# Seven quarter products in place of eight for the out-projection of an attention and feed-forward kernel on one Trainium2 core

## The chip, the cores and the metric

The kernel runs on one core of one Trainium2 chip. The metric is the device time of one execution in microseconds (us), median of several. The four executions of the kernel before took 314.61 to 314.81 us (0.06% apart). A profile records every instruction of one execution on the core's engines: PE (TensorE, matrix multiply; PEld is its weight loads), DVE (VectorE), ACT (ScalarE), POOL (GpSimd) and SP (SyncE, which here only issues DMA).

Each engine works through its own instructions in the order in which the program gives them: in the trace of the changed kernel all instructions that come from its list of words (3198 matmuls on PE, 419 instructions on DVE, 317 on ACT, 176 on POOL) start in the list's order on their engine.

## The reference

```python
def attention(q, k, v):                  # batch 8, heads 8, 576 tokens, head size 64
    scores = q @ k.T / sqrt(64)
    mask = (rel >= 0) & (rel < 64)       # sliding window, causal
    return softmax(where(mask, scores, -1e9)) @ v

def ffn(x, w_in, w_out):                 # x: 4608 x 512, w_in: 512 x 2048, w_out: 2048 x 512
    h = maximum(x @ w_in, 0)
    return (h * h) @ w_out

out = ffn(attention(q, k, v).transpose(0, 2, 1, 3).reshape(4608, 512), w_in, w_out)
```

All inputs and the output are float32; the kernels multiply fp16 and keep the products' sums in float32 tiles.

## The kernel before

The 4608 tokens are nine groups (0 to 8) of 512. A group is four chunks of 128 tokens for attention, then one up-projection of 16 slices (128 rows of h each), then one out-projection. A long list of short words gives the order of all steps on all engines; a letter after @ names the engine. The words that matter here:

- `S E M V N` (chunk): scores on PE, exponential on ACT, mask on DVE, value product on PE, normalisation on DVE.
- `U R Q` (chunk, quarter) in groups 0 and 1, `u r s` (group, slice) from group 2: up-projection on PE, relu on ACT, square.
- `O Z z`: a quarter of a token block's out-projection on PE (4 matmuls of 512 columns), eviction from PSUM (the memory that PE's results land in) on ACT, store.

```python
def up(g, f):                                   # word u: one slice, 4 matmuls of 512 columns
    hps = live["U", g, f] = ps_up.tile([P, 512], FP32, ...)      # 2 PSUM buffers
    for c in range(DMC):
        nc.tensor.matmul(hps[:], w_in_q[f // 4][:, c, ...], xT_of(g)[:, :, c, :], ...)

def relu(key, a, b):                            # words R, r
    nc.scalar.activation(out=hrelu, in_=hps[:], func=AF.Relu, scale=H_SCALE)

def square(key, a, b):                          # words Q, s: reads PSUM again, always on DVE
    nc.vector.scalar_tensor_tensor(
        out=out, in0=hps[:], scalar=0.0, in1=hr, op0=ALU.max, op1=ALU.mult)

def out_proj(g, ts, fq):                        # word O
    for f in range(4):
        nc.tensor.matmul(
            live["o", g, ts][:], h2s["h", g][:, 4 * fq + f, ts * P:(ts + 1) * P],
            w_out_q[fq][:, f, :], ...)
# ... loads, casts, attention, evictions and stores left out
```

The softmax here doesn't subtract the row's maximum and nothing guards it: scores larger than these inputs give would overflow.

## Time and profile before

| | before |
|---|---|
| time, median of 4 runs | 314.63 us (314.61 to 314.81) |
| PE, DVE, ACT, POOL busy | 95%, 59%, 52%, 32% |
| chain of waits | 81% PE |

The table of stretches of the kernel before: start and end of the stretch in us, its length, then the busy us and the instructions of PE, PEld, DVE, ACT and POOL, the granted share of PE's clock, the DMA engines' busy share and GB/s.

```profile
40.00:60.00 20.00, 18.30 (x247) 10.94 (x246) 14.21 (x34) 13.12 (x21) 9.03 (x13) 1.00 1.08 262
60.00:80.00 20.00, 18.86 (x331) 14.55 (x329) 15.19 (x36) 11.73 (x22) 8.34 (x13) 1.00 1.00 181
80.00:100.00 20.00, 18.95 (x219) 10.76 (x216) 13.68 (x27) 11.35 (x21) 10.68 (x17) 1.00 1.20 217
100.00:130.00 30.00, 28.63 (x257) 13.40 (x257) 20.61 (x46) 16.00 (x29) 11.27 (x18) 1.00 1.03 187
130.00:300.00 170.00, 170.00 (x1251) 79.14 (x1250) 92.96 (x191) 82.81 (x144) 43.42 (x69) 1.00 0.73 157
```

From 130 us PE is busy in every microsecond and is the bound. From 40 to 130 us it has small idle gaps, 5.3 us in all. Two lines of the chain of waits (start, length, what) near the end give what a matmul costs when nothing holds it up:

```profile
295.46 10.36 PE ops L440 x48
305.82 3.51 PE ops L466 x32
```

The 48 matmuls have 512 columns: 215.8 ns each. The 32 have 256 columns: 109.7 ns each. Halving the columns loses almost nothing (two of 256 take 219.4 ns, one of 512 215.8), although every matmul loads its own weights (98 ns each, on PEld beside PE). Four groups of instructions matter for the change (line, engine, operation, shapes, count; busy us and mean ns of one; idle time of the engine just before them and what ended it):

```profile
L426 DVE SCALAR_TENSOR_TENSOR h<-hps,hrelu 128x512 f16<-128x512 f32 x144 | 98.6, 689 | 86.6 <-ACT hrelu L413 86.1
L440 PE MATMUL ops<-w_out,h 128*128 128x512 f16 x560 | 140.9, 380 | 0.2 <-DVE h L426 0.2
L405 PE MATMUL hps<-xT,w_in 128*128 128x512 f16 x448 | 114.4, 380 | 1.1 <-DVE h L426 1.1
L413 ACT ACTIVATE hrelu<-hps 128x512 f32<-128x512 f32 x144 | 85.7, 599 | 97.6 <-PE hps L405 85.0
```

A warning on "PE busy": the records of matmuls overlap. The mean of one of 512 columns is 380 ns (its end is modelled by the profile), while 48 in a row took 215.8 ns each, so 380 ns is not what one costs. To see PE's real losses I add up, over the blocks of matmuls in program order, the time from one block's first matmul to the next block's first, less what the block takes at the rates above (and at the rates that blocks of other shapes show where nothing holds them up). I call the sum **PE's lost time**. It counts waits and half-clock time alike. Before, it is 26.1 us.

### The profile page before, as it was taken

How to read it: one execution, taken by the hardware profiler on the slowest of the kernel's cores; microseconds unless marked ns; L12 is line 12 of the kernel's file. 1: busy time of each engine (PE TensorE's matmuls, PEld its weight loads, DVE VectorE, ACT ScalarE, POOL GpSimd, SP SyncE). 2: the span in 40 equal slices, each digit the busy share in tenths (PEclk: the TensorE clock that was granted, in tenths of full speed). 3: DMA queues.
4: the chain of work that ended last, by engine and by line, in shares of the span. 5: the costliest groups of instructions: out<-in, count | busy, mean ns of one | idle time of the engine just before them, and what ended most of it. 6: DMA issues, size and time to landing. Idle time of an engine off the chain costs nothing.

```text
span 312.6 us, 7115 instructions
## 1 busy us (share of the span) xinstructions
PE 297.4 (95%) x2830; PEld 160.6 (51%) x2830; DVE 184.6 (59%) x402; ACT 163.4 (52%) x280; POOL 98.6 (32%) x157
## 2 busy tenths in 40 slices
PE   7599989989998999999999999999999999999995
PEld 3479844857844444444544444444444444444444
DVE  3788668596559647745764576557654855343400
ACT  2768784764556446445554565356535553444311
POOL 3443326263346216425723541333225200000000
PEclk9769999999999999999999999999999999999999
DMA  7999999899999999999989999999998022111221
GB/s 236 306 361 378 364 257 332 191 191 158 241 200 181 169 191 247 167 222 232 225 182 207 235 203 207 227 224 217 197 222 189 34 69 67 36 34 34 53 85 67
DMA packets 155569, 59.71 MB, mean 191 GB/s; under 512 B 140560, under 2 KB 146960, under 8 KB 155536
## 3 DMA queue, kind: packets, MB, share of 16 engines
q1 hardware_dynamic: 155536, 59.26, 84.1%
q8 instruction: 22, 0.36, 0.5%
q14 instruction: 11, 0.09, 0.1%
HBM read 38.80 MB, written 9.44 MB: 154 GB/s over the span
## 4 chain that ended last, share of the span: by engine, by line
PE 81%; DVE 11%; DMA 3%; ACT 2%; issue 1%; POOL 0%; SPq 0%; ACTq 0%
PE ops L440 35%; PE hps L405 29%; PE hps L396 8%; DVE pm L342 5%; PE av L353 3%; DMA kq_st<-in_q_dram 3%; PE sc L327 3%; DVE x_sb L364 2%; DVE h L426 2%; PE run_ps L285 2%; PE ops L466 1%; ACT pm L336 1%; DVE qT L291 1%; DVE rden L363 1%; ACT hrelu L413 1%
## 5 line engine op out<-in xcount | busy, mean ns | idle before, releaser
L426 DVE SCALAR_TENSOR_TENSOR h<-hps,hrelu 128x512 f16<-128x512 f32 x144 | 98.6, 689 | 86.6 <-ACT hrelu L413 86.1
L440 PE MATMUL ops<-w_out,h 128*128 128x512 f16 x560 | 140.9, 380 | 0.2 <-DVE h L426 0.2
L413 ACT ACTIVATE hrelu<-hps 128x512 f32<-128x512 f32 x144 | 85.7, 599 | 97.6 <-PE hps L405 85.0
L405 PE MATMUL hps<-xT,w_in 128*128 128x512 f16 x448 | 114.4, 380 | 1.1 <-DVE h L426 1.1
L440 PEld LDWEIGHTS <-h 128*128 128x128 f16 x560 | 52.4, 98 | 59.6 <-DVE h L426 0.3
L405 PEld LDWEIGHTS <-w_in 128*128 128x128 f16 x448 | 42.6, 98 | 51.6 <-issue 2.0
L336 ACT ACTIVATE pm<-sc 128x512 f16<-128x512 f32 x72 | 38.5, 602 | 12.8 <-PE sc L327 12.0
L270 POOL CAST v_ev<-st 128x512 f16<-128x512 f32 x31 | 19.4, 626 | 60.0 <-DMA st<-in_v_dram 27.9
L396 PE MATMUL hps<-xT,w_in 128*128 128x128 f16 x512 | 31.9, 223 | 1.1 <-DVE h L426 1.1
L364 DVE TENSOR_TENSOR x_sb<-av,rden 128x256 f16<-128x256 f32 x72 | 30.6, 425 | 2.5
L396 PEld LDWEIGHTS <-w_in 128*128 128x128 f16 x512 | 30.0, 100 | 3.3 <-issue 1.4
L448 ACT ACTIVATE osb<-ops 128x512 f32<-128x512 f32 x35 | 20.9, 600 | 18.9 <-PE ops L440 18.9
L342 DVE TENSOR_TENSOR pm<-pm,mask_inner 128x512 f16<-128x512 f16 x56 | 27.6, 523 | 0.1
L259 POOL CAST q<-st 128x512 f16<-128x512 f32 x24 | 14.9, 619 | 30.6 <-DMA st<-in_q_dram 29.5
L259 POOL CAST k<-st 128x512 f16<-128x512 f32 x28 | 17.4, 638 | 15.4 <-DMA st<-in_k_dram 15.0
L353 PEld LDWEIGHTS <-pm 128*64 128x64 f16 x576 | 13.2, 113 | 15.4 <-issue 7.8
L274 POOL COPY v_od<-v_ev 64x512 f16<-64x512 f16 x24 | 16.0, 666 | 8.1 <-DVE v_ev L270 3.7
L353 PE MATMUL av<-v_ev,pm 128*64 128x65 f16 x384 | 17.5, 202 | 0.4 <-DVE pm L342 0.2
L327 PE MATMUL sc<-qT,kT 64*128 64x64 f16 x576 | 15.2, 196 | 2.8 <-ACT qT L291 1.3
L278 POOL COPY v_od<-v_ev 64x512 f16<-64x512 f16 x24 | 15.3, 636 | 8.0 <-PE hps L396 3.5
L363 DVE RECIPROCAL rden<-av 128x4 f32<-128x4 f32 x72 | 12.6, 175 | 7.7 <-PE av L353 7.5
L327 PEld LDWEIGHTS <-kT 64*128 64x128 f16 x576 | 11.2, 98 | 8.6 <-issue 7.2
(49 smaller groups left out, 105.6 us busy)
## 6 DMA issues: line engine op xcount, KB each, us to landing
st<-in_v_dram SPq DMA_DIRECT2D x40, 256.0 KB, 4.3
out_dram<-osb SPq DMA_DIRECT2D x31, 256.0 KB, 3.2
st<-in_k_dram SPq DMA_DIRECT2D x28, 256.0 KB, 4.8
st<-in_q_dram SPq DMA_DIRECT2D x20, 256.0 KB, 4.5
w_st<-in_moe_w_in_dram SPq DMA_DIRECT2D x4, 1024.0 KB, 10.0
w_st<-in_moe_w_out_dram SPq DMA_DIRECT2D x4, 1024.0 KB, 9.8
kq_st<-in_k_dram SPq DMA_DIRECT2D x3, 1024.0 KB, 7.7
kq_st<-in_q_dram SPq DMA_DIRECT2D x3, 1024.0 KB, 9.4
```

The lines of the kernel that those rows point to most:

```text
L259: copier(e)(out=kq16(key, i // 4)[:, :, i % 4, :].rearrange("p a (b d) -> p a b d", d=D), in_=st[key, i][:].rearrange("p (a b) d -> p a b ...
L327: nc.tensor.matmul(sc[hh][:, hp, blk, :], kT[r0:r0 + 64, hp, a0:a0 + P], qTs["q", g][r0:r0 + 64, hp, a + 64 * blk:a + 64 * blk + 64], star ...
L336: nc.scalar.activation(out=pm[:], in_=live["s", i][hh][:], func=AF.Exp, scale=1.0 / float(D) ** 0.5)
L342: nc.vector.tensor_tensor(out=pms[i, hh][:], in0=pms[i, hh][:], in1=mask[:], op=ALU.min)
L353: nc.tensor.matmul(av[64 * blk:64 * blk + 64, h % 4, 0:65], pms[i, h % 2][:, h // 2, blk, :], vv[:, h, 0:65], start=True, stop=True)
L364: nc.vector.tensor_tensor(out=xs[i // 2][:, 2 * half:2 * half + 2, i % 2, :].rearrange("p c (b d) -> p c b d", d=D), in0=av[:, :, 0:D].rea ...
L396: nc.tensor.matmul(hps[:, f, :], w_in_q[fq][:, c, f * P:(f + 1) * P], xT_of(i // 4)[:, i % 4 // 2, c, a:a + P], start=(c == 0), stop=(c == ...
L405: nc.tensor.matmul(hps[:], w_in_q[f // 4][:, c, f % 4 * P:(f % 4 + 1) * P], xT_of(g)[:, :, c, :], start=(c == 0), stop=(c == DMC - 1))
L413: nc.scalar.activation(out=hrelu[:] if key == "U" else hrelu[:].rearrange("p (f t) -> p f t", t=P), in_=hps[:], func=AF.Relu, scale=H_SCALE)
L426: nc.vector.scalar_tensor_tensor(out=out, in0=hps[:], scalar=0.0, in1=hr, op0=ALU.max, op1=ALU.mult)
L440: nc.tensor.matmul(live["o", g, ts][:], h2s["h", g][:, 4 * fq + f, ts * P:(ts + 1) * P], w_out_q[fq][:, f, :], start=(fq == 0 and f == 0), ...
L448: nc.scalar.activation(out=osb[:], in_=live["o", g, ts][:], func=AF.Copy, scale=OUT_SCALE)
```

## The change

The out-projection of groups 1 to 8 becomes one level of Strassen's product (in Winograd's form): h*h and w_out are cut into 2 x 2 quarters, and seven products of sums of quarters replace eight plain ones. PE does less, DVE does sums. To make room on DVE, the squares are spread over DVE, ACT and POOL. The list of words is new throughout.

```diff
+    SQUARE = "DAAP"                    # engine of the square of slice f, by f % 4, groups 2 to 8
+    SQUARE4 = ('DDDA', 'DADA')         # groups 0 and 1
@@ def square
+        if e == "P":
+            nc.gpsimd.tensor_tensor(out=out, in0=hr, in1=hr, op=ALU.mult)
+            return
+        if e == "A":
+            nc.scalar.activation(out=out, in_=hr, func=AF.Square)
+            return
+    def w_sum(n, h, e):                # word ta: 4 sums of w_out, in halves of 128 x 1024 fp16, once
+    def h_sum(g, n, h, e):             # word sa: 4 sums of h*h, in halves, for every group
+        if n == 1:
+            a, b = h_view(g, 1, 0, h), h_view(g, 1, 1, h)
+        elif n == 2:
+            a, b = s_of(g, 1)[:, f], h_view(g, 0, 0, h)
+        ...
+        combine(s_of(g, n)[:, f], a, b, ALU.add if n == 1 else ALU.subtract, e)
+    def product(g, n, m):              # word p: 8 matmuls of 256 columns; n = 1 to 7, m = 0, 1
+    def part(g, n):                    # word va: PSUM to SBUF with a sum (n = 0 on ACT, else DVE)
+    def whole(g, c):                   # word vc: last sum of an output quarter, on DVE
+    def store_whole(g, c):             # word vz: 256 KB store
@@ the list of words: all of group 1 onwards reordered; excerpt at the end of group 2
+    sa2.1.0@D s2.14 sa2.3.0@D p2.1.0 r2.15
+    sa2.2.0@D u3.0 s2.15 dv17 sa2.3.1@D sa2.4.0@D p2.1.1 r3.0 cv16@P sa2.1.1@D dv18 u3.1 va2.0
+    s3.0 cn16@P sa2.2.1@D u3.2 r3.1 dv19 vc1.1 s3.1 sa2.4.1@D p2.2.0 ...
```

(Cuts: scaling constants, pools, some of them now with fewer buffers, views, loads and the rest of the list.) Relu's scale is adapted so that every engine's square comes out alike.

## The prediction

> **Bound now.** The tensor engine. The table of stretches shows PE 30.0 of 30 us busy in each stretch from 150 to 300 us, granted clock 1.00; the chain of waits is 81% PE. Before 120 us PE idles some 10 us, mostly the first 9.4. DVE (59%), ACT (52%), POOL (32%) have room.
>
> Rates, from the chain of waits: 48 out-projection matmuls of 512 columns took 10.36 us (215.8 ns each); the 32 of 256 columns in the last block 3.51 us (109.7 ns each), though each loads new weights (98 ns, hidden).[...]
>
> **Removed.** Groups 1 to 8 take 496 x 215.8 ns + 32 x 109.7 ns = 110.5 us of PE. After: 8 x 7 x 2 x 8 = 896 matmuls of 256 columns x 109.7 ns = 98.3 us. Saving 12.2 us, 1.5 per group.
>
> **Added and moved** (durations from the groups of instructions).
> - DVE: 96 of 144 squares leave (0.69 us: -66). In come 64 h sums and 8 w sums of 128x1024 fp16 (the 128x512 fp16 mask took 0.42 us median; estimate 0.7 us alone, 0.8 to 1.0 with POOL in the way: 55 to 70 us) and 56 combines from PSUM (0.69 like the square: 39). Net 185 to about 220 us.
> - ACT: 68 squares (0.6), 31 fewer evictions, 8 first parts: 163 to about 190 us.
> - POOL: 28 squares of 128x512 fp32[...].
> None gets near PE.
>
> **Critical path.** From about 110 us PE is the chain, so nearly all 12.2 us come out. I take back:
> - Tail, +1.4 us: the last 0.38 us eviction and 128 KB store (2.1 us) become a 0.69 us combine and a 256 KB store (3.2 us).
> - Border of groups 1 and 2 (80 to 120 us), +1 us: out-projection of group 1 filled PE between attention steps of chunks 8 to 11; in the new order no product comes before those are nearly done.
> - Product stalls, +0.7 us: every fourth slice goes ACT relu, POOL square, DVE sums; POOL's in-order queue also waits for load DMAs (72 us in all, single waits to 5.8), so a square can stick behind a cast. Most sums have 3 to 4 us of other PE work before use, so small stalls, mostly in group 2 and in group 8, where no up-projection is left to fill.
> Loads (DMA busy to about 242 us) are unchanged and attention keeps its absolute times, so they should not bind.
>
> **Prediction:** 314.6 - 12.2 + 3.1 = 305.5 us; range 302.3 to 309.5. Faster by over 2%: 0.83; within 2%: 0.16; slower: 0.01.
>
> **Signs that each step is right.** Products at 110 ns each (0.88 us for eight); PE busy about 285 us, 30 of 30 in stretches after 130 us, still about 80% of the chain of waits; h sums 0.7 to 1.0 us; last matmul to end about 4.5 us against 3.3; PE idle before products under 3 us in total.
>
> **What would make it wrong.** (a) Products slower than 110 ns, or PSUM's two buffers freed late by combines queued behind sums on DVE; (b) POOL squares of 1.5 us or more, or stuck behind casts that wait for DMA, so that PE waits every group; (c) h sums of 1.1 us and more[...]: DVE at 240 us, on the chain; (d) the reordered first 100 us, with w sums on DVE, gaining or losing 2 to 3 us by itself.

Three passages are cut out of it, where marked: a rule about matmuls and a figure for POOL's squares, with the total for POOL that rests on it, and a mechanism for slow sums; none was shown by this case. No term of the sum goes with them: -12.2 us, and 1.4 + 1.0 + 0.7 = 3.1 us taken back, give 305.5 us. But "None gets near PE" has no figure left for POOL. That POOL slows DVE's sums is an estimate with this behind it: in the trace before, a mask takes 0.41 to 0.43 us with no POOL instruction beside it (24 masks) and 0.41 to 1.11 us with one (48).

## The result, and the profile after

| | before | after |
|---|---|---|
| time, median of 4 runs | 314.63 us (314.61 to 314.81) | 309.55 us (308.32 to 310.15) |
| ratio, 95% interval | | 0.983 (0.980 to 0.986) |
| span of the profiled run | 312.6 us | 308.1 us |
| PE, DVE, ACT, POOL busy | 95, 59, 52, 32% | 94, 69, 60, 45% |

(A ratio here is the mean time of one kernel's runs over that of the other's runs of the same rounds, so not quite the ratio of the medians. Executions over 1.5% slower than the fastest of the same kernel are left out of the means.) The gain is 5.1 us, 1.7%, where 9.1 us were forecast; the median lies 0.05 us above the forecast range. The forecast had put 0.83 on a gain of over 2%; the measured gain is within 2%.

Groups of instructions after, the new ones and the up-projection (L417):

```profile
L417 PE MATMUL hps<-xT,w_in 128*128 128x512 f16 x448 | 111.9, 379 | 1.5 <-DVE h L450 1.5
L445 POOL TENSOR_TENSOR h<-hrelu 128x512 f16<-128x512 f32 x28 | 31.7, 1131 | 80.9 <-ACT hrelu L429 80.9
...
L580 PE MATMUL pps<-w_sum,h_sum 128*128 128x256 f16 x384 | 48.6, 273 | 0.9 <-DVE h_sum L540 0.9
L450 DVE SCALAR_TENSOR_TENSOR h<-hps,hrelu 128x512 f16<-128x512 f32 x48 | 32.8, 687 | 23.8 <-ACT hrelu L429 23.6
...
L540 DVE TENSOR_TENSOR h_sum<-h 128x1024 f16<-128x1024 f16 x32 | 23.9, 764 | 27.0 <-PE pps L580 26.1
```

The h sums (0.76 us) and the products cost what was forecast: in the chain of waits the last 56 product matmuls took 6.13 us (109.5 ns each). POOL squares took 1.13 us.

```profile
297.98 6.13 PE pps L580 x56
```

The up-projection waits 1.5 us for DVE squares (L417). Such waits are not new: before there were 1.1 us in L405 and as much in L396. The table of stretches after:

```profile
40.00:60.00 20.00, 16.98 (x217) 9.37 (x215) 18.06 (x41) 11.58 (x19) 10.33 (x12) 1.00 1.04 250
60.00:80.00 20.00, 18.57 (x333) 16.54 (x331) 13.99 (x33) 14.81 (x26) 8.17 (x13) 0.91 0.84 166
80.00:100.00 20.00, 18.29 (x236) 13.50 (x232) 13.99 (x21) 13.28 (x25) 9.95 (x13) 1.00 1.08 212
100.00:130.00 30.00, 28.62 (x318) 18.08 (x318) 23.90 (x51) 18.70 (x34) 18.96 (x26) 1.00 1.03 194
130.00:300.00 170.00, 169.18 (x1600) 112.13 (x1599) 111.89 (x221) 101.68 (x177) 75.09 (x96) 1.00 0.79 162
```

After 130 us PE is still busy 169.2 of 170 us, as forecast. The losses lie before: at 40 to 60 us DVE is at 90% and PE idles 3 us, and from 60 to 80 us the granted clock is 0.91. PE's lost time by stretch, for seven of the profiled runs:

| lost us in | 0-10 | 10-40 | 40-60 | 60-80 | 80-100 | 100-130 | 130 to end | sum |
|---|---|---|---|---|---|---|---|---|
| before | 8.0 | 6.9 | 2.7 | 1.7 | 2.0 | 2.5 | 2.3 | 26.1 |
| after | 7.9 | 8.3 | 4.0 | 4.3 | 2.7 | 2.4 | 3.4 | 33.1 |
| no_sums | 8.0 | 7.1 | 2.4 | 5.1 | 2.1 | 0.9 | 3.5 | 29.1 |
| g1_classic | 8.0 | 7.8 | 2.1 | 1.3 | 1.4 | 4.9 | 3.8 | 29.2 |
| squares_only | 7.9 | 7.3 | 2.4 | 1.2 | 1.7 | 1.5 | 2.4 | 24.4 |
| fill_only | 8.2 | 8.0 | 4.8 | 2.1 | 2.3 | 1.9 | 3.2 | 30.6 |
| tuned3 | 8.0 | 7.2 | 2.3 | 1.6 | 2.7 | 0.8 | 2.3 | 24.9 |

The books balance. From before to after, PE's matmuls cost 12.2 us less, 7.0 us more are lost, and the time from the last matmul to the end grew from 3.3 to 4.0 us: -12.2 + 7.0 + 0.7 = -4.5, and the spans differ by 4.5. (The stretches are fixed in time, so a row's entries shift a little against each other; the sums don't.)

Not all of the 7.0 us is the new order's. Of it, 1.4 us stand at 10 to 40 us, before the first sum (43.9 us). There the clock record of this execution has PE at half clock (granted clock 0.50) for 13.65 us, from 10.40 us, and that of the kernel before for 10.24 us, from 11.28 us; the mean granted clock from 10 to 40 us is 0.77 and 0.83. fill_only has 0.77 too and has lost as much by 40 us (16.2 us); no_sums and tuned3, with the same words up to there, have 0.83 and lose 15.1 and 15.2. So about 1 us of the profiled run's shortfall differs from execution to execution.

What stands in the gaps? First, 40 to 60 us, lines of the timeline after (start, length, engine, line, operation, shapes; in brackets idle before it and what ended that):

```profile
43.91 1.74 DVE L540 TENSOR_TENSOR w_sum<-w_out 128x1024 f16<-128x1024 f16 x2
45.57 1.10 DVE L540 TENSOR_TENSOR w_sum<-w_out,w_sum 128x1024 f16<-128x1024 f16 x1
...
49.80 0.41 DVE L282 CAST v_ev<-st 128x512 f16<-128x512 f32 x1
50.28 1.08 POOL L286 COPY v_od<-v_ev 64x512 f16<-64x512 f16 x1 [4.16 <-DVE v_ev L282]
...
51.41 0.19 PE L365 MATMUL av<-v_od,pm 128*64 128x65 f16 x1 [0.62 <-POOL v_od L286]
```

DVE computes w sums ahead of a cast of v; POOL waits 4.16 us for that cast before it can copy; PE waits for POOL, three times in this stretch; such waits take 1.5 us in the whole run, 0.4 before. A second kind of place, at 115 to 121 us, where group 2 ends and group 3 begins:

```profile
117.22 1.53 DVE L540 TENSOR_TENSOR h_sum<-h,h_sum 128x1024 f16<-128x1024 f16 x1
118.67 1.09 DVE L540 TENSOR_TENSOR h_sum<-h 128x1024 f16<-128x1024 f16 x1
119.68 0.68 DVE L450 SCALAR_TENSOR_TENSOR h<-hps,hrelu 128x512 f16<-128x512 f32 x1
...
120.42 0.81 PE L417 MATMUL hps<-xT,w_in 128*128 128x512 f16 x3 [0.71 <-DVE h L450]
```

The square of group 3's first slice stands on DVE behind h sums of group 2. As a DVE square reads PSUM, the up-projection's buffer is not free until then, and PE waits. A third, at 64 to 68 us, among the attention steps of chunks 8 to 11:

```profile
64.11 3.04 ACT L348 ACTIVATE pm<-sc 128x512 f16<-128x512 f32 x6
...
66.72 0.19 PE L339 MATMUL sc<-qT,kT 64*128 64x64 f16 x1 [0.17 <-ACT pm L348]
67.67 0.40 PE L339 MATMUL sc<-qT,kT 64*128 64x64 f16 x15 [0.77 <-DVE x_sb L376]
68.01 1.54 PE L408 MATMUL hps<-xT,w_in 128*128 128x128 f16 x16
```

Here PE has only small matmuls that wait on each other through ACT and DVE. In the kernel before, out-projection blocks of group 1 stood among them. Right after it the clock record shows 3.41 us at half clock (0.50 from 68.4 to 71.8 us): the last line's 16 matmuls take 1.54 us where others of their kind take 1.05. The matmuls that start in this window are spaced over 3.3 us, where the rates above give 1.8: about 1.5 us of the 4.3 lost at 60 to 80 us (an estimate from this trace). The kernel before has no such window between 22 us and its last matmul. What brings the half clock is not shown: PE idled 1.12 us from 60 to 68.4 us, at most 0.77 us at a stretch from 64 us on.

### The profile page after: what moved, and what is told of

Its sections match the earlier page's. It is cut to its first block, busy times and chain, and to the rows that moved or that the text cites. A ratio compares the mean times of both kernels' runs of the same rounds, so it can differ in the third digit from the quotient of the medians.

```text
span 308.1 us, 7884 instructions
## 1 busy us (share of the span) xinstructions
PE 289.9 (94%) x3198; PEld 200.3 (65%) x3198; DVE 211.7 (69%) x437; ACT 185.7 (60%) x319; POOL 139.2 (45%) x186
## 4 chain that ended last, share of the span: by engine, by line
PE 75%; DVE 12%; DMA 5%; ACT 3%; POOL 1%; issue 1%; SPq 0%; DVEq 0%; ACTq 0%
PE pps L580 31%; PE hps L417 29%; PE hps L408 7%; DVE pm L354 4%; PE av L365 3%; DVE h_sum L540 3%; DMA kq_st<-in_q_dram 3%; DMA st<-in_v_dram 2%; PE sc L339 2%; DVE x_sb L376 2%; DVE h L450 1%; ACT pm L348 1%; PE ops L464 1%; ACT hrelu L429 1%; PE run_ps L297 1%
## 5 line engine op out<-in xcount | busy, mean ns | idle before, releaser
L417 PE MATMUL hps<-xT,w_in 128*128 128x512 f16 x448 | 111.9, 379 | 1.5 <-DVE h L450 1.5
L445 POOL TENSOR_TENSOR h<-hrelu 128x512 f16<-128x512 f32 x28 | 31.7, 1131 | 80.9 <-ACT hrelu L429 80.9
L417 PEld LDWEIGHTS <-w_in 128*128 128x128 f16 x448 | 42.1, 98 | 35.7 <-issue 1.9
L580 PEld LDWEIGHTS <-h_sum 128*128 128x128 f16 x512 | 49.3, 98 | 16.4 <-DVE h_sum L540 1.7
L580 PE MATMUL pps<-w_sum,h_sum 128*128 128x256 f16 x384 | 48.6, 273 | 0.9 <-DVE h_sum L540 0.9
L450 DVE SCALAR_TENSOR_TENSOR h<-hps,hrelu 128x512 f16<-128x512 f32 x48 | 32.8, 687 | 23.8 <-ACT hrelu L429 23.6
L580 PEld LDWEIGHTS <-h 128*128 128x128 f16 x384 | 37.0, 98 | 11.9 <-DVE osp L598 0.3
L448 ACT ACTIVATE h<-hrelu 128x512 f16<-128x512 f32 x68 | 43.0, 633 | 2.0
L540 DVE TENSOR_TENSOR h_sum<-h 128x1024 f16<-128x1024 f16 x32 | 23.9, 764 | 27.0 <-PE pps L580 26.1
L580 PE MATMUL pps<-w_out,h 128*128 128x256 f16 x256 | 32.5, 273 | 0.0
L376 DVE TENSOR_TENSOR x_sb<-av,rden 128x256 f16<-128x256 f32 x72 | 30.6, 425 | 2.5
L282 POOL CAST v_ev<-st 128x512 f16<-128x512 f32 x32 | 23.0, 723 | 15.8 <-DMA st<-in_v_dram 13.9
L598 DVE SCALAR_TENSOR_TENSOR osp<-pps,ws 128x512 f32<-128x512 f32 x32 | 21.9, 683 | 7.4 <-PE pps L580 7.4
L591 DVE SCALAR_TENSOR_TENSOR ws<-pps,ws 128x512 f32<-128x512 f32 x24 | 16.4, 684 | 12.6 <-PE pps L580 12.6
```

Source lines behind the costliest of these rows:

```text
L376: nc.vector.tensor_tensor(out=xs[i // 2][:, 2 * half:2 * half + 2, i % 2, :].rearrange("p c (b d) -> p c b d", d=D), in0=av[:, :, 0:D].rea ...
L417: nc.tensor.matmul(hps[:], w_in_q[f // 4][:, c, f % 4 * P:(f % 4 + 1) * P], xT_of(g)[:, :, c, :], start=(c == 0), stop=(c == DMC - 1))
L445: nc.gpsimd.tensor_tensor(out=out, in0=hr, in1=hr, op=ALU.mult)
L448: nc.scalar.activation(out=out, in_=hr, func=AF.Square)
L450: nc.vector.scalar_tensor_tensor(out=out, in0=hps[:], scalar=0.0, in1=hr, op0=ALU.max, op1=ALU.mult)
L540: eng.tensor_tensor(out=out, in0=in0, in1=in1, op=op)
```

## The experiments

Two causes are proposed, and a third is a rival to both. **A**: DVE's in-order queue holds the sums ahead of work that PE needs. **B**: the new order leaves PE without other work among the attention steps of chunks 8 to 11. **C**: the sums cost in the steady part, because DVE and POOL slow each other. All results but no_sums's are correct.

### no_sums: what do the sums cost?

```diff
- every word sa and ta taken out of the list
-                lhs = s_of(g, {3: 4, 5: 1, 6: 2, 7: 3}[n])[:, f, m * P:(m + 1) * P]
+                a, b = {3: (0, 1), 5: (1, 1), 6: (1, 1), 7: (0, 0)}[n]
+                lhs = h2s["h", g][:, 8 * b + f, (2 * a + m) * P:(2 * a + m + 1) * P]
-                rhs = t_of({4: 4, 5: 1, 6: 2, 7: 3}[n])[:, f]
+                row, col = {4: (1, 0), 5: (0, 1), 6: (1, 1), 7: (1, 1)}[n]
+                rhs = w_view(row, col, f // 4)[:, f % 4]
```

> The changed kernel with all 64 h sums and 8 w sums taken out; the products read quarters of h and w_out in their place, so matmuls, their order and all combines stay and the result is wrong on purpose. Theory A (the 4 us missing from the forecast are PE idle before 130 us, made by DVE's in-order queue: w sums among the masks of chunks 4 to 7, h sums ahead of the squares of group 2 at 84 to 90 and 115 to 120 us): 305 to 306.5 us, and PE idle between 40 and 130 us falls by 3 us or more. Rival B (the new order of the first groups, with no out-projection between the attention steps of chunks 8 to 11, costs the time whatever DVE does): 308.5 us or more. Rival C (sums cost in the steady stretches[...]): a gain of over 2 us between 130 and 300 us.

Measured: 305.19 us (303.89 to 305.87), ratio to before 0.970 (0.967 to 0.972); the result is wrong. So the sums cost about 4 us of the changed kernel's 309.5. (In the two profiles 1.2 of the 4.0 us between the spans stand at 10 to 40 us, before any sum; but the two runs of mean clock 0.983 also differ by 4.4 us, 308.32 and 303.89.) The loss went where A says: 40 to 60 us from 4.0 to 2.4 lost us, 100 to 130 us from 2.4 to 0.9. After 130 us nothing was gained (3.4 and 3.5): C falls. But 60 to 80 us kept its loss (5.1), half-clock window included (mean granted clock 0.91, as after): A alone is not the whole cause. POOL's same 186 instructions took 128.2 us in place of 139.2; and of the changed kernel's 72 sums, the 34 with no POOL instruction beside them took 0.67 to 0.69 us, the other 38 0.68 to 1.53. So sums and POOL do slow each other; it just doesn't reach PE after 130 us. PE's waits from 40 to 130 us, in us, show what the sums held up, and that order, with one square moved, can free it (tuned3, below, has all the sums):

| PE waits for | before | after | no_sums | tuned3 |
|---|---|---|---|---|
| POOL's copies of v | 0.4 | 1.5 | 0.2 | 0.2 |
| DVE squares | 2.2 | 1.5 | 0.2 | 0.3 |
| h sums | | 0.9 | | 0 |
| the cast of w_out on DVE | 0 | 0.5 | 0.2 | 0.1 |

The squares' waits of the kernel before go with the spread of the squares (0.3 us in squares_only); the sums brought most of them back.

### g1_classic: the old product for group 1

```diff
+ the list of the kernel before up to group 2's last slice, with O1.0.0 to O1.3.3
+ ta words after s2.6 to s2.13
+ the new list from the h sums of group 2 on
- all sa1, p1, va1, vc1, vz1 words
```

> Group 1 by the old eight quarter products in the old kernel's order up to its last slice, Strassen from group 2 on, w sums spread over the squares of group 2. Costs 64 x 215.8 - 112 x 109.7 ns = 1.5 us of PE. Theory A and rival B both expect the front to be as in the kernel before, so 305.5 to 307.5 us: faster than the changed kernel although it multiplies more. Rival C: 311 us, since the steady stretches stay.

Measured: 307.09 us (306.53 to 307.76), ratio 0.976 (0.974 to 0.978). It beats the changed kernel by some 2 us although PE multiplies 1.5 us more. Lost time from 40 to 100 us falls from 11.0 to 4.8 us. C's 311 us is refuted again. One new gap of 2.5 us stands at 113.5 to 116.0 us, at slice 2 of group 3, again behind h sums on DVE, and a half-clock window follows it (116.7 to 120.1 us; mean granted clock 0.94 from 100 to 130 us).

### dve_squares: all squares back on DVE

```diff
-    SQUARE = "DAAP"
-    SQUARE4 = ('DDDA', 'DADA')
+    SQUARE = "DDDD"
+    SQUARE4 = ('DDDD', 'DDDD')
```

> The changed kernel with all 144 squares on DVE again. DVE then has some 212 + 96 x 0.69 = 278 us of work. Theory A (DVE's queue makes the loss): clearly slower than the changed kernel, 313 to 325 us, and now also PE idle in the steady stretches. Rival B: little change, 309 to 311 us.

Measured: 326.26 us (325.77 to 327.39; one slow run 330.91), ratio 1.036 (1.034 to 1.038). Even slower than expected. DVE is busy only 265 us of 326, 81%, and yet it ruins the kernel: PE loses 18.3 us after 130 us (2.3 before, 3.4 after), mostly ahead of up-projection slices (L417 waits 13.0 us for DVE squares in the whole run, 1.5 after). An engine at 81% is not "off the critical path" if what PE needs next is at the end of its queue.

### squares_only: the kernel before with nothing but the spread squares

```diff
+    SQUARE = "DAAP"
+    SQUARE4 = ('DDDA', 'DADA')
+    (square on POOL or ACT as in the change; list of words of the kernel before)
```

> The kernel before with the squares on three engines and nothing else. All theories: PE is the bound, so 313.8 to 315.2 us; DVE about 120 us busy. If squares on POOL stuck behind casts that wait for DMA cost time, it would be 316 us or more; if the squares on DVE cost time in the front before, 313 us or less.

Measured: 312.76 us (312.64 to 312.88), ratio 0.994 (0.993 to 0.996). This part alone gains 1.9 us. The three theories had not expected it; the expectation names the case (squares on DVE that cost time in the front). DVE, at 126 us instead of 185, delays PE less in the first 130 us (lost 14.1 us from 10 to 130 us, before 15.8). So of the changed kernel's 5.1 us, Strassen's product, on top of the spread squares, gave only about 3.2. And 28 squares on POOL cost PE nothing here (2.4 lost us after 130 us).

### paad: which engine squares which slice

```diff
-    SQUARE = "DAAP"
+    SQUARE = "PAAD"
```

> The changed kernel with one word altered: slices f = 0, 1, 2, 3 (mod 4) of groups 2 to 8 are squared by POOL, ACT, ACT, DVE in place of DVE, ACT, ACT, POOL. The first square of a group no longer stands on DVE behind the h sums of the group before, so the PSUM buffer of slice 0 is freed by ACT's relu; and the last square, which the sums wait for, is DVE's own. Theory A (DVE's order): the gap of 0.9 us at slice 2 of group 3 (and the small ones at other groups) goes, 308.3 to 309.3 us. If the squares' engines don't matter: 309.5 us.

Measured: 308.83 us (307.82 to 309.48), ratio 0.978 (0.974 to 0.983). The before runs of this batch were less steady (314.4 to 317.3), and the intervals overlap with the changed kernel's: **inconclusive**. In the trace the gap at slice 2 of group 3 is gone, but a new one of 0.74 us (0.58 of it idle) stands in group 8, before product 2.

### warm_gap: dummy matmuls against the half-clock window

```diff
+ W4 ahead of S11        (4 matmuls on zeros into a free PSUM buffer)
```

> The changed kernel with four matmuls on zeros (0.86 us of PE) put before the scores of chunk 11, where PE idles 0.95 us anyway. Tests the half-clock window of 3.4 us at 68 us that the changed kernel's profile shows and the kernel before lacks. If the window comes of PE's idling there and costs what half a clock for 3.4 us may cost: window gone and 308 to 309 us. If it costs nothing: 309.5 us or slightly more, window gone or not.

Measured: 308.42 us (307.98 to 308.76), ratio 0.977 (0.973 to 0.981). The window is gone from this profile (granted clock 1.00 from 60 to 80 us, 0.91 in the changed kernel's). The gain is not clear of noise against the changed kernel's 0.983 (0.980 to 0.986). Whether the order there brings the window is not shown: paad, which has the changed kernel's, has 0.91 from 60 to 80 us in the table of its trace, but 0.981 over its whole span, and the two don't fit. A hint on the cost: the changed kernel's runs of mean clock 0.970 and 0.971 took 310.15 and 309.83 us, those of 0.981 and 0.983 took 309.27 and 308.32. But the profiled one of them (0.971) has both this window and the longer half clock at the start, so the 1.2 us between the pairs belong to both. That the window costs up to some 1 us when it comes is **suggested, not shown**.

### tuned: sums out of the way (a first attempt at a better kernel)

```diff
- ta1.0 to ta4.1 among the attention words of chunks 4 to 7
+ ta1, ta2, ta3 after N11.1, Q6.0, Q6.2; ta4.0 and ta4.1 after va1.1 and va1.2
+ u2.2 ahead of p1.6.0; the square of chunk 7, slice row 2, on ACT; SQUARE = "PAAD"
```

> The changed kernel, Strassen in groups 1 to 8, with paad's assignment, the w sums moved from 44 to 62 us to idle places of DVE at 77 to 84 us and later, the square of chunk 7, slice row 2 on ACT, and slice 2 of group 2's up-projection ahead of product 6 of group 1. Theory A: 306 to 308 us, PE idle from 40 to 60 us down by 1 us and from 80 to 92 us down by 1.5 us; the 60 to 72 us stretch stays (rival B's share). Rival B alone: 308.5 to 309.5 us.

Measured: 307.32 us, runs 306.3 to 307.32 (a fourth, slow, 311.03), ratio 0.973 (0.968 to 0.978). As A expects: lost time from 40 to 60 us fell from 4.0 to 2.7 us, and from 80 to 92 us PE is busy 11.80 us in place of 10.29. The stretch from 60 to 80 us stayed at 4.8 us with its half-clock window (mean granted clock 0.91), as expected of B's share.

### classic_paad: the two together: a miss

```diff
  g1_classic, and
-    SQUARE = "DAAP"
+    SQUARE = "PAAD"
```

> Group 1 by the old product (g1_classic, 307.1 us) with paad's assignment. In g1_classic one gap remained, 2.7 us at slice 2 of group 3 at 112 us, waiting for a DVE square behind four h sums, with a half-clock window after it. Theory A: the gap and the window go, 303.3 to 305 us. If that gap has another cause: 306.5 to 307.5 us.

Measured: 309.82 us (309.42 to 309.98), ratio 0.982 (0.977 to 0.987), on another chip than g1_classic (0.976, 0.974 to 0.978): by the ratios 1.8 us slower, though the intervals touch, where 2 to 4 us of gain were expected. The gap behind the DVE square did go, and another came, with a half-clock window after it (120.3 to 123.7 us; mean granted clock 0.94 from 100 to 130 us). Timeline of classic_paad on POOL, SP and PE:

```profile
108.15 1.51 POOL L451 TENSOR_TENSOR h<-hrelu 128x512 f16<-128x512 f32 x1 [3.43 <-ACT hrelu L435]
109.61 2.09 POOL L277 CAST q<-st 128x512 f16<-128x512 f32 x2
...
112.14 4.21 SPq L328 DMA_TRANSPOSE qT<-q  x1
...
119.01 0.64 PE L345 MATMUL sc<-qT,kT 64*128 64x64 f16 x32 [1.97 <-DMA qT<-q]
```

PE waits 1.97 us for the transposed q of the next group. That DMA needs casts on POOL, and POOL's queue now holds the squares at other places, each waiting for its relu (this one for 3.43 us). In g1_classic such a wait (3.50 us) ended 2.7 us earlier, and the DMA was issued at 110.60 us. The forecast had feared squares stuck behind casts. What the trace shows is the reverse: casts stuck behind a square. No further run tested it.

### after_again and fill_only: other work among the attention steps

```diff
  fill_only:
- O0.2.3 ahead of Tq2.0, O0.3.3 ahead of U4.0
+ O0.2.3 after U4.2, O0.3.3 after V8.1 (evictions Z0.2, Z0.3 later)
```

> The changed kernel once more, to stand on the same chip and beside the same runs of the kernel before as the next two. All theories: 308.3 to 310.2 us, as in its first four runs; a half-clock window at 65 to 72 us in some of them.

> The changed kernel with two blocks of group 0's out-projection (4 matmuls each) moved from ahead of the attention of chunks 8 to 11 into it: one after the third up-projection block, one ahead of the scores of chunk 11; their evictions follow later. No work is added or taken, DVE's order stays. Rival B (PE lacks other work between the attention steps): PE idle from 60 to 80 us down from 4.3 us to 3 us or less, no half-clock window there, 307.3 to 308.7 us. If the gaps there come from ACT or DVE alone, so that the fill only shifts them: 309 to 310 us.

Measured on one chip: after_again 308.86 us (median of three runs, 308.08 to 309.63), ratio 0.982 (0.979 to 0.985); fill_only 307.0 us (306.36 to 307.39), ratio 0.976 (0.973 to 0.978). One execution of after_again, the profiled one, took 418.56 us at a mean granted clock of 0.653 and is left out as slow; what caused that no run here shows. Two blocks of four matmuls, moved by a few microseconds, gain about 2 us: B is shown. Lost time from 60 to 80 us is 2.1 us (4.3 after), and the half-clock window there is gone. PE in that stretch, after and then fill_only (busy us, instructions, clock, DMA share, GB/s):

```profile
60.00:80.00 20.00, 18.57 (x333) 0.91 0.84 166
```

```profile
60.00:80.00 20.00, 19.09 (x360) 1.00 0.91 165
```

### tuned2: both attempts together, another miss

```diff
  tuned, and
+ fill_only's move; r8.15 s8.15 ahead of sa8.3.0
```

> tuned (w sums late, paad's assignment) with fill_only's move and, in the last group, the last square ahead of the sums on DVE (0.74 us of PE idle before product 2 of group 8 in tuned). Theory A and rival B together, their gains adding: 304.5 to 306 us, PE idle after the first 10 us under 20 us in all (after: 25.2, before: 18.1). If the two gains are the same microseconds: 306.5 to 307.5 us.

Measured: 307.48 us (306.01 to 309.89), ratio 0.978 (0.973 to 0.983), not clear of the changed kernel's. The gains did not add. Lost time from 40 to 80 us is 5.0 us (after: 8.3), but 80 to 100 us now loses 4.2 us, where group 1's product 6 reaches its sums too early, and after 130 us it loses 5.7 us (after: 3.4). Why "PAAD" loses more after 130 us than "DAAP" in tuned and tuned2 (4.6 and 5.7 against 3.2 to 3.5) I did not settle; classic_paad's POOL queue is a candidate.

### tuned3: order, and one square on ACT

```diff
  fill_only (SQUARE = "DAAP" as in the change), and
+ ta words as in tuned; the square of chunk 7, slice row 2, on ACT
+ p1.7.0 p1.7.1 ahead of p1.6.0       (product 7's sums are ready earlier than product 6's)
+ s3.0 ahead of sa2.1.1               (the square that frees the PSUM buffer first)
+ u7.11 ahead of V33.0, p6.7.1 ahead of V34.0
```

> fill_only (307.0 us) with further moves of order and nothing added: the w sums late as in tuned, the square of chunk 7, slice row 2 on ACT, product 7 of group 1 ahead of product 6, the first square of group 3 ahead of group 2's h sums on DVE, and in group 7 an up-projection slice and half a product ahead of the value matmuls of chunks 33 and 34. The squares' engines stay DVE, ACT, ACT, POOL. Theory (PE's idle time in the first 130 us is one of order, and each gap named in a trace can be filled): 303.5 to 306 us; PE idle from 40 to 60 us under 3 us (4.9 in fill_only), the gap of 0.9 us at slice 2 of group 3 gone, from 240 to 250 us under 0.8 us (1.5). If the gains overlap, as in tuned2: 306.5 to 307.5 us.

Measured: **302.37 us** (5 runs, 301.63 to 303.67), ratio to before 0.963 (0.960 to 0.965). This beats both kernels: 12.2 us under the kernel before, and by the ratios 2% under the changed kernel (0.963 / 0.982 = 0.980). It is better than expected. The same stretches in its profile:

```profile
40.00:60.00 20.00, 18.69 (x291) 11.87 (x290) 16.15 (x36) 12.96 (x22) 9.63 (x13) 1.00 1.08 266
60.00:80.00 20.00, 19.42 (x335) 16.95 (x333) 16.97 (x38) 16.14 (x30) 9.02 (x14) 1.00 1.12 191
80.00:100.00 20.00, 18.53 (x224) 11.74 (x222) 18.70 (x36) 13.59 (x26) 13.89 (x18) 1.00 1.07 203
100.00:130.00 30.00, 30.00 (x306) 19.38 (x305) 22.95 (x45) 18.72 (x33) 17.93 (x25) 1.00 1.06 213
```

Save for 80 to 100 us, PE is as busy as in the kernel before or more, at a granted clock of 1.00, with the same operations on DVE but one square (212.2 us busy, after 211.7) and the same buffers, so neither the amount of DVE's work nor the smaller pools can be what cost the changed kernel its gain. PE's lost time is 24.9 us, below the kernel before's 26.1, so as much as the 12.2 us of saved multiplication reaches the clock. The spread squares have their part in it: squares_only loses 24.4 us, and against its span (310.9 us) tuned3 gains 11.0. The chain of waits by engine, after and then tuned3:

```profile
PE 75%; DVE 12%; DMA 5%; ACT 3%; POOL 1%; issue 1%; SPq 0%; DVEq 0%; ACTq 0%
```

```profile
PE 84%; DVE 7%; ACT 4%; DMA 3%; issue 1%; POOL 0%; SPq 0%; ACTq 0%
```

How the last 4.6 us from fill_only divide among the five moves was not measured one by one; of these moves only the late w sums and the square on ACT (in tuned) had a run, and there with others.

## Why the prediction was right or wrong

- **"The tensor engine" as the bound, and the saving of 12.2 us: right.** Product matmuls took 109.5 ns each against 109.7 forecast; the matmul terms of the two kernels differ by 12.2 us; tuned3 gained as much, some of it from the spread squares.
- **Sizes of the added work: right.** h sums 0.76 us (0.7 to 1.0), DVE 212 us (220), ACT 186 (190). POOL squares took 1.13 us (1.04 without the sums, in no_sums), well under the 1.5 us of (b), and POOL was busy 139 us.
- **Steady part: right.** PE 169.2 of 170 us after 130 us; lost time there rose by 1.1 us. 0.8 us of it are PE's waits for normalisations of the last attention steps (about 248 to 252 us); tuned3, which puts other PE work there, loses 2.3 us, as the kernel before.
- **"Tail, +1.4 us": too large.** From the last matmul to the end went from 3.3 to 4.0 us, +0.7.
- **"Border of groups 1 and 2 (80 to 120 us), +1 us": the mechanism was right, the place was off.** It stands at 60 to 80 us, where lost time rose by 2.6 us, some 1.5 of them by the half-clock window that was not thought of. Moving two blocks of matmuls (fill_only) gained about 2 us.
- **"Product stalls, +0.7 us": the step that failed.** I costed the waits of products for their sums. The page shows only 0.9 us of that. The larger waits, 3.5 us from 40 to 130 us, were of *other* PE work for *other* work that stood behind the sums: value matmuls at 51 to 55 us (1.5 us, casts behind w sums), up-projection slices at 87 and 120 us (1.5 us, squares behind h sums) and 0.5 us for a cast of w_out. Without the sums the three are 0.6 us. no_sums puts the cost of the sums in all at about 4 us, nearly all before 130 us. I had listed w sums in the first 100 us only among the things that could go wrong (d), with no term in the sum.
- **"None gets near PE": true and misleading.** I compared busy totals. dve_squares shows the trap: DVE at 81% busy cost 17 us against the changed kernel.
- **"A square can stick behind a cast": not seen in PE's waits.** squares_only lost nothing to it after 130 us; in classic_paad it was the reverse.
- **Loads "should not bind": held** in the changed kernel's steady part; a transposed load did bind once the order was changed (classic_paad, 1.97 us).
- **Not thought of:** the spread of the squares gains 1.9 us by itself (squares_only), and a half-clock window can stand among PE's waits (a mean granted clock of 0.91 from 60 to 80 us in after, no_sums, paad and tuned, of 0.94 from 100 to 130 us in g1_classic and classic_paad; what brings it is not shown, its cost is only suggested).

In sum: -12.2 us of matmuls, +7.0 us lost, +0.7 us tail gives -4.5 us of span (5.1 us by the medians), against -12.2 + 3.1 forecast. Of the +7.0, about 1 us is the longer half clock at the start of this execution and about 1.5 us the half-clock window at 68 us.

## What to carry to other kernels

When a change moves work from the bounding engine to one with room, don't only compare busy totals: for every engine, walk its queue and ask what the bounding engine needs that now stands *behind* the new work, above all what frees its PSUM buffers. New work that is not urgent (sums for a later product) goes behind the urgent, and stretches where the bounding engine waits on a chain of other engines need filler from elsewhere, so it pays to keep some back. Here the same arithmetic took 309.6 us in one order and 302.4 in another (with one square moved to another engine).
